# Decay attention in blocks of 64 tokens with a state in mid-chunk, and the second products of hidden group 0 in units of two banks

## The chip, the cores and the metric

The program runs on one core of a Trainium2 chip. The metric is the device time of one execution in microseconds (us), the median of three runs. TensorE (PE) does the matrix products, VectorE (DVE), ScalarE (ACT) and GpSimd (POOL) the elementwise work, and SyncE (SP) issues the DMA transfers. PEld stands for TensorE's weight loads.

## The reference

Two parts, cut to what matters. First an attention with a decay per head, in blocks of tokens with a running state (2 sequences of 768 tokens, 8 heads of 64 channels):

```python
for b in range(nb):                                  # block = 64 tokens
    intra = einsum('bhic,bhjc->bhij', qb, kb) * Dmask          # lam**(i-j), lower triangle
    intra = einsum('bhij,bhjd->bhid', intra, vb)
    inter = einsum('bhid,bhde->bhie', qb * lam_pow, kv_state)  # lam**(i+1)
    out[:, :, sl] = intra + inter
    kv_state = lam_block * kv_state + einsum('bhsd,bhse->bhde', kb * rev_pow, vb)
```

Its output is laid out as 1536 tokens by 512 channels. Two layers follow, each `(act(x @ w_in)) @ w_out` with 2048 hidden units, the first with Mish and the second with SiLU. The result does not depend on the size of the block, as long as the powers of lam are those of the distance between two tokens.

## The kernel before

**Numbers.** The products of the two layers are done in fp32r with each operand split into a high and a low part (`xh`, `xl`, `wh`, `wl`, `gh`, `gl`): three products for one, so 12 matmuls of 128x512 for one 128-wide slice of hidden units and one `t` (512 tokens). A weight is split by two passes on ACT (L95, L96), two on DVE (L123, L127), a cast on ACT (L167) and a subtraction on POOL (L168). The attention's products are plain fp32. Each of these matmuls stands in the trace as two.

**Attention.** There are N = 12 chunks of 128 tokens, six of a sequence. `emit_S` makes the scores of one chunk for 4 pairs of heads (8 matmuls, contraction over 64 channels, 128x128 each, into two banks `s`), and DVE multiplies them by `dmask` into `sm`. `emit_state` makes `pc` = keys times values (8 matmuls with 64 columns), which DVE adds to the decayed `state`. `emit_px` makes the state's part of the output and `emit_out` the scores' part (8 matmuls with 128 columns each, in one bank `px`), which ACT copies to `xh` and DVE completes with `xl`. ACT and POOL make the decayed keys `kd`, POOL the decayed queries `qd`.

**Order.** All engines' instructions stand in the order in which Python emits them (a manual schedule), and each engine runs its own list in that order. Chunks 0 to 3 (PH = 4) are done alone at the start. Then 12 steps follow (`t` over 3 groups of 512 tokens, `f` over the 4 hidden slices of group 0). Step i emits `emit_h(t, f)` (the first product of a slice, `ph`), then chunk n = i + 4 as long as n < 12, then, from step 2 on, the second product of the slice two steps back (`emit_o`, 12 matmuls into four banks `po` that stay open over four slices and are copied by ACT at the end, `evac`). Steps 0 to 7 hold a chunk, steps 8 to 11 none. After that the seven other groups of hidden units run as a list of items, with a faster algorithm (`Block`) for two of the three token groups. Its operands are sums of blocks of x, which `make_sums` lists and `run_sums` emits from step 8 on: 13 DVE operations of 128x1024.

**PSUM** has eight banks: two for `ph` (`ps_h`), four for `po` (`ps_o`), two for the attention (`ps_a`).

Of the kernel before, what the change touches and what calls it, by code (L numbers as in the profile page):

```python
# [17 lines left out]
def decay_attention_mish_silu_kernel(  # L18
# [8 lines left out]
    nc = tc.nc  # L27
# [5 lines left out]
    C = P  # L33
    NP = H // 2
# [13 lines left out]
    accp = ctx.enter_context(tc.tile_pool(name="accp", bufs=1))  # L48
# [5 lines left out]
    ps_o = ctx.enter_context(tc.tile_pool(name="ps_o", bufs=4, space=PSUM))  # L54
# [137 lines left out]
    ps_a = actx.enter_context(tc.tile_pool(name="ps_a", bufs=2, space=PSUM))  # L192


    states = [ac.tile([P, NP, D], F32, name=f"state{i}") for i in range(2)]

    def warm(n):
# [9 lines left out]
    unit = ac.tile([P, C], F32, name="unit")  # L207
    nc.gpsimd.memset(unit, 0.0)
    nc.gpsimd.affine_select(
        out=unit, in_=unit, pattern=[[1, C]], base=1 - C, channel_multiplier=1, compare_op=ALU.not_equal, fill=1.0  # L210
    )
# [27 lines left out]
    load_x()  # L239
    load_w(0, 0)  # L240
    load_x()
    load_w(1, 0)

    qd, kd, ss, sm, pxs = {}, {}, {}, {}, {}

    def emit_kd(n):
        if n < N and n % CPS < CPS - 1:
# [10 lines left out]
    def emit_qd(n):  # L258
        if n < N and n % CPS > 0:
            t = qd[n] = at.tile([P, NP, C], F32, tag="qd", name="qd")  # L260
            nc.gpsimd.tensor_tensor(out=t, in0=nat[n][1], in1=lamrow, op=ALU.mult)  # L261

    def emit_S(n, pool, tag, mask=True):
        if n >= N:
            return
        kT, qT, kn, vn = nat[n]
        ss[n] = [pool.tile([P, NP, C], F32, tag=tag, name=f"s{hh}") for hh in range(2)]
        for p in range(NP):
            for hh in range(2):
                r = slice(64 * hh, 64 * hh + 64)  # L270
                nc.tensor.matmul(ss[n][hh][:, p, :], lhsT=kT[r, p, :], rhs=qT[r, p, :], start=True, stop=True)  # L271
        if mask:
            emit_mask(n)

    def emit_mask(n):
        t = sm[n] = at.tile([P, 2, NP, C], F32, tag="sm", name="sm")
        for hh, s in enumerate(ss.pop(n)):
            nc.vector.tensor_tensor(out=t[:, hh], in0=s, in1=dmask[:, hh], op=ALU.mult)

    def emit_decay(n):  # L280

        if 0 < n % CPS < CPS - 1:
            nc.gpsimd.tensor_tensor(
                out=states[(n + 1) % 2], in0=states[n % 2],
                in1=lamrow[:, :, C - 1 : C].to_broadcast([P, NP, D]), op=ALU.mult,
            )

    def emit_state(n):
        c = n % CPS
        if c == CPS - 1:  # L290
            return
        vn = nat[n][3]
        early = PH <= n < PH + LAG
        pc = (ps_o if early else ps_a).tile([P, NP, D], F32, tag="o" if early else "a", name="pc")
        for p in range(NP):
            for hh in range(2):
                h = 2 * p + hh
                nc.tensor.matmul(  # L298
                    pc[64 * hh : 64 * hh + 64, p, :], lhsT=kd[n][:, h, :], rhs=vn[:, h, :], start=True, stop=True
                )  # L300
        new = states[(n + 1) % 2]
        if c == 0:
            nc.vector.tensor_copy(new, pc)
        else:
            nc.vector.tensor_tensor(out=new, in0=pc, in1=new, op=ALU.add)

    def emit_px(n):
        px = pxs[n] = (ps_h if n < PH else ps_a).tile([P, NP, C], F32, tag="h" if n < PH else "a", name="px")
        if n % CPS > 0:
            for p in range(NP):  # L310
                for hh in range(2):
                    r = slice(64 * hh, 64 * hh + 64)
                    nc.tensor.matmul(  # L313
                        px[r, p, :], lhsT=states[n % 2][r, p, :], rhs=qd[n][r, p, :],
                        start=(p == 0), stop=False, skip_group_check=True,
                    )

    def emit_out(n):
        px, vn = pxs.pop(n), nat.pop(n)[3]
        for p in range(NP):  # L320
            for hh in range(2):
                nc.tensor.matmul(  # L322
                    px[64 * hh : 64 * hh + 64, p, :], lhsT=vn[:, 2 * p + hh, :], rhs=sm[n][:, hh, p, :],
                    start=(n % CPS == 0 and p == 0), stop=(p == NP - 1), skip_group_check=True,
                )
        xslots.append(held.pop(("x", n)))
        xh, xl = x_tile(n // CPB)
        o = slice((n % CPB) * C, (n % CPB + 1) * C)
        nc.scalar.copy(xh[:, :, o], px)
        nc.vector.tensor_tensor(out=xl[:, :, o], in0=px, in1=xh[:, :, o].bitcast(F32), op=ALU.subtract)  # L330
# [10 lines left out]
    def bank(name):  # L341
        nbank[0] += 1
        if len(late) > 2 and nbank[0] % 2:
# [45 lines left out]
    def emit_o(t, n, first, last):  # L389
# [4 lines left out]
        if first:  # L394
            po[t] = [ps_o.tile([P, T], F32, tag="o", name="po") for j in range(4)]
# [19 lines left out]

    PIECES = [(j, slice(0, T)) for j in range(3)] + [(3, slice(0, T // 2)), (3, slice(T // 2, T))]
# [15 lines left out]
    def evac(mm, g, t):  # L432
        if g == 0:
            accs[mm, t] = (accp if t == 0 else late[1]).tile([P, 4, T], F32, tag="acc", name="acc")
# [42 lines left out]
    def make_sums(pool):  # L477
# [8 lines left out]
        fz = late[1].tile([P, 4, T], F32, tag="acc", name="fz")[:, 0:2]  # L486
        add, sub = ALU.add, ALU.subtract
        summing.extend([
            [tt(fx, a21[0], a22[0], add), tt(fx, fx, a21[1], add)],
            [tt(fx, fx, a22[1], add), cast(0, fx), tt(fz, *a11, add)],  # L490
            [low(0, fx), tt(fx, fx, fz, sub), cast(1, fx)],
            [tt(fz, fz, a21[0], sub), low(1, fx)],
            [tt(fz, fz, a21[1], sub), cast(2, fz), tt(fx, a12[0], fx, sub)],
            [low(2, fz), tt(fx, fx, a12[1], add), cast(3, fx)],
# [72 lines left out]
    loads = ["x", (2, 0), "x", (0, 1), "x", (3, 0), (1, 1), "x", (2, 1), (3, 1), "x", (4, 0), (5, 0)]  # L567
# [11 lines left out]
    spread = ps_a.tile([P, H], F32, tag="a", name="spread")  # L579
# [5 lines left out]
    dmask = ac.tile([P, 2, NP, C], F32, name="dmask")  # L585
    ages = dmask[:, :, :, C - 1]
    lamrow = ac.tile([P, NP, C], F32, name="lamrow")
    last = ac.tile([P, H], F32, name="last")
    nc.gpsimd.tensor_tensor(out=last, in0=lams, in1=unit[:, 0:1].to_broadcast([P, H]), op=ALU.mult)
    powers = ps_a.tile([P, NP, C], F32, tag="a", name="powers")  # L590
    for hh in range(2):
        for p in range(NP):
            h = H - 1 - (2 * p + hh)
            nc.vector.tensor_tensor_scan(
                out=dmask[:, hh, p], data0=lams[:, h : h + 1].to_broadcast([P, C]), data1=unit, initial=0.0,
# [3 lines left out]
    emit_S(0, ps_o, "o")  # L599
    for hh in range(2):  # L600
        for p in range(NP):
            h = H - 1 - (2 * p + hh)
            nc.tensor.matmul(
                powers[64 * hh : 64 * hh + 64, p, :], lhsT=last[:, h : h + 1].to_broadcast([P, 64]),
                rhs=dmask[:, hh, p], start=True, stop=True,
            )
    emit_kd(0)
    nc.scalar.copy(lamrow, powers)
    emit_qd(1)
    emit_state(0)  # L610
    emit_px(0)
    emit_out(0)
    emit_decay(1)
    emit_kd(1)
    emit_S(1, ps_o, "o")
    emit_px(1)
    emit_state(1)
    for n in range(PH):
        if n > 1:
            emit_state(n)  # L620
            emit_px(n)
        if n:
            if n < PH - 1:
                emit_S(n + 1, ps_o, "o")
            if n == PH - 2:
                run_split(2)
            emit_out(n)
            if n == PH - 1:
                emit_S(n + 1, ps_o, "o")
            if n == PH - 1:  # L630
                emit_kd(n + 1)
            emit_qd(n + 1)
            emit_decay(n + 1)
        if n == 1:
            for half in ((0, 0), (1, 0), (2, 0), (0, 1), (3, 0), (1, 1), (2, 1), (3, 1), (4, 0), (5, 0)):
                split_w(*half, half[0] > 3)
        pump()
        if n != PH - 2:
            run_split(2)
        run_pre(1 + (n == PH - 1), 0)  # L640
        run_parts()
        if n < PH - 2:
            emit_kd(n + 2)
        tick[0] += 1

    for i, (t, f) in enumerate(steps):
        n = i + PH
        if n == N:
            actx.close()
            late.append(ctx.enter_context(tc.tile_pool(name="ringt", bufs=2)))  # L650
            late.append(ctx.enter_context(tc.tile_pool(name="accq", bufs=NB - 1)))
            fctx = ExitStack()
            make_sums(fctx.enter_context(tc.tile_pool(name="ps_f", bufs=1, space=PSUM)))
# [4 lines left out]
        run_parts()  # L658
        if i < LAG or n >= N:
            run_split(2)  # L660
        emit_h(t, f, f == 0)
        if n < N:
            if i == 1:
                run_parts()
            emit_state(n)
            emit_px(n)
            if i < LAG:
                emit_S(n + 1, ps_o, "o")
            emit_out(n)
# [143 lines left out]
```

## Time and profile before

| | |
|---|---|
| time, median of 3 runs | 563.49 us (563.44 to 563.55) |
| profiled execution | 563.52 us, span 561.7 us |
| granted TensorE clock | 1.00 in every stretch |
| PE busy | 556.1 us (99%) |
| first `ph` product begins | 22.83 us |
| chunk steps end, step 8 begins | 90.68 us |

The span runs from the first to the last instruction; 1.8 us of the profiled execution lie outside it. Busy time on PE counts matmuls from their start to their modelled end, and they overlap, so that a busy PE does not say how fast it goes: for that the distance from one batch of matmuls to the next is read.

### The profile page before, as it was taken

Reading aid. Unit: us, or ns where it says so; the run is one execution under the profiler, and the core shown is the slowest. Engines: PE = TensorE matmul, PEld = TensorE weight load, DVE = VectorE, ACT = ScalarE, POOL = GpSimd, SP = SyncE. Lnnn points to the kernel's source line nnn. Section 1 sums busy time; section 2 is a strip of 40 time slices with the busy share of each in tenths; the row PEclk is TensorE's granted clock in tenths of the full one; section 3 lists DMA queues with packets and bytes.
Section 4 is the critical chain, followed back from the end, with each engine's and each line's share of the span. In section 5 each row is a group of like instructions: output and inputs, shape, how many; then the busy total and the mean of one; then the engine's idle time right before and its main releaser. Section 6 shows DMA issues by size and latency. Waiting matters only on the chain.

```text
span 561.7 us, 7611 instructions
## 1 busy us (share of the span) xinstructions
PE 556.1 (99%) x2956; PEld 454.6 (81%) x2956; DVE 312.3 (56%) x458; ACT 286.9 (51%) x538; POOL 164.1 (29%) x137
## 2 busy tenths in 40 slices
PE   9999999999999999999999999999999999999997
PEld 6877778887887888888888788888888888888885
DVE  4866536764467684446669882344634654455222
ACT  4676422863562763455546973656443654355120
POOL 4554512123034122312462652302322312303000
PEclk9999999999999999999999999999999999999999
DMA  8986600122022231212311141212320322100203
GB/s 301 405 271 224 226 1 1 49 93 84 1 76 75 69 118 39 75 39 80 109 38 37 41 150 41 70 39 87 101 75 2 109 78 73 41 0 1 75 7 144
DMA packets 14597, 49.77 MB, mean 89 GB/s; under 512 B 1633, under 2 KB 1889, under 8 KB 14561
## 3 DMA queue, kind: packets, MB, share of 16 engines
q1 hardware_dynamic: 14560, 49.29, 25.8%
q8 instruction: 23, 0.38, 0.3%
q14 instruction: 14, 0.11, 0.1%
HBM read 46.14 MB, written 3.15 MB: 88 GB/s over the span
## 4 chain that ended last, share of the span: by engine, by line
PE 95%; DMA 2%; SPq 1%; DVE 1%; POOL 0%; ACT 0%; issue 0%; DVEq 0%; POOLq 0%
PE po L409 46%; PE ph L382 20%; PE b L519 10%; PE a L519 7%; PE e L519 3%; PE c L519 3%; DMA xslot<-x 2%; PE px L322 2%; PE s L271 2%; PE px L313 1%; PE pc L298 1%; SPq L226 1%; DVE acc L440 1%; POOL wl L168 0%; POOL qd L261 0%
## 5 line engine op out<-in xcount | busy, mean ns | idle before, releaser
L168 POOL TENSOR_TENSOR wl<-dec,wh 128x512 fp32r<-128x512 f32 x64 | 85.2, 1333 | 270.6 <-ACT wh L167 233.6
L409 PE MATMUL po<-gh,wh 128*128 128x512 f32 x192 | 75.9, 395 | 0.1
L409 PE MATMUL po<-gh,wl 128*128 128x512 f32 x192 | 75.0, 390 | 0.1
L409 PE MATMUL po<-wh,gh 128*128 128x512 f32 (+1 forms) x193 | 75.0, 388 | 0.0
L409 PE MATMUL po<-wh,gl 128*128 128x512 f32 (+1 forms) x193 | 74.9, 388 | 0.0
L409 PE MATMUL po<-wl,gh 128*128 128x512 f32 (+1 forms) x193 | 74.9, 388 | 0.0
L366 DVE TENSOR_TENSOR gl<-ph,gh 128x512 fp32r<-128x512 f32 x40 | 27.5, 688 | 71.8 <-ACT ph L365 71.8
L365 ACT ACTIVATE gh<-ph 128x512 fp32r<-128x512 f32 x40 | 23.9, 598 | 80.5 <-PE ph L382 80.3
L382 PE MATMUL ph<-xh,wh 128*128 128x512 f32 x160 | 62.8, 395 | 0.0
L123 DVE SCALAR_TENSOR_TENSOR dec<-dec,slot 128x512 uint32<-128x512 uint32 x64 | 52.5, 820 | 17.4 <-ACT slot L96 16.0
L382 PE MATMUL ph<-xl,wh 128*128 128x512 f32 x160 | 60.8, 389 | 0.0
L440 DVE TENSOR_TENSOR acc<-po,acc 128x512 f32<-128x512 f32 (+1 forms) x73 | 45.7, 676 | 23.8 <-PE po L409 23.8
L167 ACT CAST wh<-dec 128x512 fp32r<-128x512 f32 x64 | 39.6, 619 | 37.4 <-DVE dec L127 37.0
L168 POOL TENSOR_TENSOR tl<-t,th 128x512 fp32r<-128x512 f32 x28 | 38.3, 1377 | 65.4 <-ACT th L167 63.9
L409 PE MATMUL po<-gl,wh 128*128 128x512 f32 x192 | 51.4, 389 | 0.0
L127 DVE SCALAR_TENSOR_TENSOR dec<-slot,dec 128x512 uint32<-128x512 uint32 x64 | 48.9, 764 | 1.7
L409 PEld LDWEIGHTS po<-gh,wh 128*128 128x128 f32 x192 | 36.0, 188 | 9.6 <-DVE acc L440 1.4
L382 PE MATMUL ph<-xh,wl 128*128 128x512 f32 x160 | 43.7, 389 | 0.0
L95 ACT ACTIVATE dec<-slot 128x512 f32<-128x512 f32 x64 | 42.7, 667 | 2.1 <-DMA slot<-w 2.1
L96 ACT ACTIVATE slot<-slot 128x512 uint32<-128x512 uint32 x64 | 42.7, 667 | 0.0
L409 PEld LDWEIGHTS po<-wh,gh 128*128 128x128 f32 x193 | 36.2, 188 | 7.7 <-issue 0.3
L409 PEld LDWEIGHTS po<-wl,gh 128*128 128x128 f32 x193 | 36.2, 188 | 7.5
(119 smaller groups left out, 946.7 us busy)
## 6 DMA issues: line engine op xcount, KB each, us to landing
slot<-w SPq DMA_DIRECT2D x64, 512.0 KB, 3.6
xslot<-x SPq DMA_DIRECT2D x24, 512.0 KB, 8.1
out<-acc SPq DMA_DIRECT2D x11, 256.0 KB, 2.1
out<-acc SPq DMA_DIRECT2D x2, 128.0 KB, 1.9
factors<-lam SPq DMA_DIRECT2D x1, 0.0 KB
```

The lines of the kernel that those rows point to most:

```text
L95: nc.scalar.activation(decs[n, i].bitcast(F32), high.bitcast(F32), AF.Copy, scale=2.0**-112)
L96: nc.scalar.activation(low, low, AF.Copy, scale=TOP3, bias=2.0**-21 - 0.5)
L123: nc.vector.scalar_tensor_tensor(out=d, in0=d, scalar=3, in1=low, op0=ALU.logical_shift_left, op1=ALU.bitwise_or)
L127: nc.vector.scalar_tensor_tensor(out=d, in0=high, scalar=0x80000000, in1=d, op0=ALU.bitwise_and, op1=ALU.bitwise_or)
L167: nc.scalar.copy(hi, f)
L168: nc.gpsimd.tensor_tensor(out=lo, in0=f, in1=hi.bitcast(F32), op=ALU.subtract)
L365: nc.scalar.activation(to, ps, AF.Mish if mm == 0 else AF.Silu)
L366: later.append(lambda: nc.vector.tensor_tensor(out=gl, in0=ps, in1=gh.bitcast(F32), op=ALU.subtract))
L382: nc.tensor.matmul(ph, lhsT=wi[wsel][:, kk * P : (kk + 1) * P], rhs=xt[xsel][:, kk, :], start=(i == 0), stop=(i == 3 * KD - 1),)
L409: nc.tensor.matmul(po[t][j][:, c], lhsT=lhsT, rhs=rhs, start=(first and wsel + gsel == 0), stop=(last and gsel == 1 and c.stop == T),)
L440: nc.vector.tensor_tensor(out=acc[:, j, c], in0=po[t][j][:, c], in1=acc[:, j, c], op=ALU.add)
L519: nc.tensor.matmul(self.b[dst], lhsT=w[ws][:, kk * P : (kk + 1) * P], rhs=x[xx][:, kk, :], start=(start and i == 0), stop=(i == 5), skip_g ...
```

## The change

Attention works on half chunks: L = 64 tokens. All its matmuls contract over 64 rows into 64 columns of output partitions and move 64 columns, so that each uses one quarter of TensorE's array, and there are 16 of them where there were 8. The state is kept at the end of the chunk (`states`) and in its middle (`mids`); POOL makes `fades`, the state decayed by half a chunk. `emit_pc` makes both halves' `pc`, `emit_state` the next state, `emit_intra` the scores' part and `emit_inter` the states' part of `px`. The first product of the chunk that begins a sequence has no state in its first half only. In the steps the order is `emit_h`, intra, `pc`, then the second product, inter, and the scores of the next chunk.

The second products of group 0 are emitted as `emit_u`: a unit takes two slices and two of the four output blocks, 12 matmuls into two banks, which are emptied at once (ACT copies the first two units of a `t` to `acc`, DVE adds the others to it). `ps_o` has two banks, and the sums get PSUM for both of their operands and 12 smaller groups in another order. At the start the whole of chunk 3 is loaded ahead of the first weights, and the weights' order differs by one place.

```diff
-    def emit_S(n, pool, tag, mask=True):
+    def emit_S(n, pair=False):
...
         for p in range(NP):
+            for c in range(2):
+                for hh in range(2):
+                    r = inner[hh]
+                    nc.tensor.matmul(
+                        s[hh][rows[c], p], lhsT=kT[r, p, rows[c]], rhs=qT[r, p, half[c]], start=True, stop=True
+                    )
...
+    def emit_pc(n):
+        c0, ends = n % CPS == 0, n % CPS == CPS - 1
...
+        for p in range(NP):
+            for c in range(1 if ends else 2):
+                for hh in range(2):
+                    h = 2 * p + hh
+                    nc.tensor.matmul(
+                        pc[inner[hh], c, p], lhsT=kd[n][rows[c], h], rhs=vn[rows[c], h], start=True, stop=True
+                    )
+        mid = mids[n % 2]
+        if c0:
+            nc.vector.tensor_copy(mid, pc[:, 0])
+        else:
+            nc.vector.tensor_tensor(out=mid, in0=pc[:, 0], in1=fades[n % 2], op=ALU.add)
...
+    def emit_inter(n):
+        for c in (1, 0)[: 1 if n % CPS == 0 else 2]:
+            state = (states, mids)[c][n % 2]
+            for p in range(NP):
+                for r in inner:
+                    nc.tensor.matmul(
+                        pxs[n][1][c][r, p], lhsT=state[r, p], rhs=qd[n][r, p, c],
...
+    def emit_u(t, u, between=None):
+        js, fs = (2 * (u % 2), 2 * (u % 2) + 1), (2 * (u // 2), 2 * (u // 2) + 1)
...
+        order = ((0, 0, 0), (0, 0, 1), (1, 0, 0), (0, 1, 0), (1, 0, 1), (1, 1, 0))
+        passes = [(fs[k], j, ws, gs) for k, ws, gs in order for j in range(2)]
+        for i, (f, j, ws, gs) in enumerate(passes):
+            if between and i == len(passes) // 2:
+                between()
...
+        def leave():
+            for j in range(2):
+                if u < 2:
+                    nc.scalar.copy(acc[:, js[j], :], banks[j])
+                else:
+                    nc.vector.tensor_tensor(out=acc[:, js[j], :], in0=banks[j], in1=acc[:, js[j], :], op=ALU.add)
...
+            leave = emit_u(*divmod(i - LAG, 4), close if ends else None)
+            if n < N and not ends:
+                emit_inter(n)
+            if n < N:
+                emit_S(n + 1, True)
+            if n < N and not ends:
+                emit_out(n)
+            if n < N:
                 run_parts()
+            leave()
...
-        run_sums(1 + (i > len(steps) - 3))
+        run_sums(1 + (n < N + 2))
```

On PE, step 4 (chunk 8) reads as follows before, from the end of `ph` on; S of the next chunk closes it.

```order
L382 MATMUL ph<-xl,wh_281 128x512 x4
L298 MATMUL pc<-xslot_100,kd 64x64 x8
L313 MATMUL px<-qd,state_98 64x128 x8
L322 MATMUL px<-sm,xslot_100 64x128 x8
L409 MATMUL po<-gh,wh_610 128x512
...
L409 MATMUL po<-gl,wh_610 128x512 x4
L271 MATMUL s_836<-xslot_101 128x128
L271 MATMUL s_837<-xslot_101 128x128
```

The same step of the change (`px` from `sm` is intra, `px` from `mid` and `state` is inter):

```order
L428 MATMUL ph<-xl,wh_399 128x512 x4
L346 MATMUL px<-sm,xslot_104 64x64 x16
L313 MATMUL pc<-xslot_104,kd 64x64 x16
L474 MATMUL pu<-gh,wh_803 128x512 x2
L474 MATMUL pu<-gl,wh_803 128x512 x2
L474 MATMUL pu<-gh,wh_930 128x512 x2
L474 MATMUL pu<-gh,wl_804 128x512 x2
L474 MATMUL pu<-gl,wh_930 128x512 x2
L474 MATMUL pu<-gh,wl_931 128x512 x2
L357 MATMUL px<-qd,mid_100 64x64 x8
L357 MATMUL px<-qd,state_98 64x64 x8
L296 MATMUL s<-xslot_105 64x64 x16
```

The attention's products stand in two blocks of one shape where they stood in two blocks of four shapes, and the state's part has moved behind the second product, next to S.

On ACT, in step 2 before, the cast of the weights of the fourth slice (`wh_481`) that step 3's `ph` reads, and what stands around it:

```order
L365 ACTIVATE gh<-ph 128x512
L365 ACTIVATE ph<-ph 128x512
L329 CAST xh<-px 128x4x128
L256 ACTIVATE kd<-xslot_103,dmask 128x64 x4
L167 CAST wh_481<-dec 128x512
```

In the change the same cast is that of `wh_796`:

```order
L411 ACTIVATE gh<-ph 128x512
L411 ACTIVATE ph<-ph 128x512
L168 CAST wh_689<-dec 128x512
L264 ACTIVATE kd<-xslot_107,dmask 128x64 x4
L375 CAST xh<-px 128x4x128
L168 CAST wh_796<-dec 128x512
```

It is still behind the copy of the chunk's `px`, but that `px` is now finished only after the second product.

On DVE, from step 8 on before (`t` are weights' sums, `fx` and `fz` the sums of x, `gl` the low part that the second product reads):

```order
L430 TENSOR_TENSOR fx<-xh 128x1024
L430 TENSOR_TENSOR fx<-fx,xl 128x1024
L153 TENSOR_TENSOR t_1087<-dec 128x256
L153 TENSOR_TENSOR t_1087<-dec,t_1087 128x256
L366 TENSOR_TENSOR gl<-ph,gh 128x512
L430 TENSOR_TENSOR fx<-fx,xl 128x1024
L430 TENSOR_TENSOR fz<-xh,xl 128x1024
L366 TENSOR_TENSOR gl<-ph,gh 128x512
```

And in the change, from step 8 to the start of step 10:

```order
L484 TENSOR_TENSOR acc<-pu,acc 128x512 x2
L505 TENSOR_TENSOR fx<-xh 128x1024
L505 TENSOR_TENSOR fx<-fx,xl 128x1024
L154 TENSOR_TENSOR t_1587<-dec 128x256
L154 TENSOR_TENSOR t_1587<-dec,t_1587 128x256
L412 TENSOR_TENSOR gl<-ph,gh 128x512
L484 TENSOR_TENSOR acc<-pu,acc 128x512 x2
L505 TENSOR_TENSOR fx<-fx,xl 128x1024
L505 TENSOR_TENSOR fz<-xh,xl 128x1024
...
L412 TENSOR_TENSOR gl<-ph,gh 128x512
```

Each step's sums now stand behind two additions that wait for the end of the step's unit.

## Rows read from the trace of the kernel before

**Rows 1.** Page: the span, and each engine's busy time.

```profile
span 561.7 us, 7611 instructions
PE 556.1 (99%) x2956; PEld 454.6 (81%) x2956; DVE 312.3 (56%) x458; ACT 286.9 (51%) x538; POOL 164.1 (29%) x137
```

**Rows 2.** Page: the chain that ended last, by engine.

```profile
PE 95%; DMA 2%; SPq 1%; DVE 1%; POOL 0%; ACT 0%; issue 0%; DVEq 0%; POOLq 0%
```

**Rows 3.** Windows: busy PE, PEld, DVE, ACT, POOL; PEclk, DMA share, GB/s.

```profile
0.00:22.83 22.83, 21.55 (x286) 16.57 (x286) 13.75 (x28) 11.89 (x31) 10.42 (x18) 1.00 0.90 341
22.83:44.07 21.24, 21.24 (x209) 16.88 (x209) 14.82 (x22) 14.85 (x34) 11.90 (x13) 1.00 0.82 281
90.52:139.96 49.44, 49.31 (x217) 40.47 (x216) 32.27 (x38) 27.87 (x49) 12.51 (x9) 1.00 0.20 64
```

**Rows 4.** Chain in order of time: start us, length us, what.

```profile
22.83 2.94 PE ph L382 x12
...
44.07 2.95 PE ph L382 x12
...
53.74 2.95 PE ph L382 x12
56.69 0.62 PE pc L298 x16
57.30 1.02 PE px L313 x16
58.32 1.02 PE px L322 x16
59.35 2.97 PE po L409 x12
62.31 1.09 PE s L271 x16
...
82.74 2.95 PE ph L382 x12
...
90.68 2.72 PE ph L382 x12
```

**Rows 5.** Timeline of PE at the start: start us, busy us, shape, count.

```profile
14.10 1.09 PE L322 MATMUL px<-sm,xslot 128*64 128x128 f32 x16
15.02 0.64 PE L298 MATMUL pc<-xslot,kd 128*64 128x64 f32 x16
15.59 1.09 PE L313 MATMUL px<-qd,state 64*64 64x128 f32 x16
```

**Rows 6.** Timeline of PE, chunk 0's `pc` among `powers`.

```profile
8.52 0.27 PE L603 MATMUL powers<-dmask,last 128*64 128x128 f32 x1
8.52 0.22 PE L298 MATMUL pc<-xslot,kd 128*64 128x64 f32 x1
8.63 0.27 PE L603 MATMUL powers<-dmask,last 128*64 128x128 f32 x1
```

**Rows 7.** Timeline of the first weights and chunk 3 at the start.

```profile
13.20 0.42 DVE L305 TENSOR_TENSOR state<-pc,state 128x256 f32<-128x256 f32 x1 [0.30 <-PE pc L298]
...
17.65 1.06 ACT L256 ACTIVATE kd<-xslot,dmask 128x64 f32<-128x64 f32 x4 [0.67 <-DMA xslot<-x]
...
19.32 0.69 ACT L95 ACTIVATE dec<-slot 128x512 f32<-128x512 f32 x1
...
21.18 0.62 ACT L167 CAST wh<-dec 128x512 fp32r<-128x512 f32 x1 [0.60 <-DVE dec L127]
21.78 0.59 ACT L329 CAST xh<-px 128x512 fp32r<-128x512 f32 x1
```

**Rows 8.** Timeline of DVE from step 8 on.

```profile
89.01 0.68 DVE L366 TENSOR_TENSOR gl<-ph,gh 128x512 fp32r<-128x512 f32 x1
89.61 0.41 DVE L153 TENSOR_TENSOR t<-dec 128x256 f32<-128x256 f32 x1
...
91.66 1.23 DVE L430 TENSOR_TENSOR fx<-fx,xl 128x1024 f32<-128x1024 f32 x1
```

More of the change, by code (lines that the diff above doesn't have):

```diff
@@ L280, in emit_decay @@
[L280 to L285, printed above, removed]
-            )
[L288 to L291, printed above, removed]
+        t = sm[n] = at.tile([P, 2, NP, L], F32, tag="sm", name="sm")
+        if pair:
+            both = ps_a.tile([P, 2, T], F32, tag="xy", name="s")[:, :, 0 : NP * L].rearrange("q hh (p i) -> q hh p i", p=NP)
+            s = [both[:, hh] for hh in range(2)]
+        else:
+            s = [ps_o.tile([P, NP, L], F32, tag="o", name=f"s{hh}") for hh in range(2)]
@@ new lines, in emit_state, with emit_intra @@
+    def emit_state(n):
+        pc, mid = pcs.pop(n), mids[n % 2]
+        if n % CPS == CPS - 1:
+            return
+        for p in range(NP):
+            nc.vector.scalar_tensor_tensor(
+                out=states[(n + 1) % 2][:, p], in0=mid[:, p], scalar=lamrow[:, p, L - 1 : L], in1=pc[:, 1, p],
+                op0=ALU.mult, op1=ALU.add,
+            )
+        emit_fade(n + 1)
+    def emit_intra(n):
+        if n < PH and n % 2 == 0:
+            pxs[n] = None, [ps_h.tile([P, NP, L], F32, tag="h", name=f"px{i}") for i in range(2)]
+        else:
+            both = ps_a.tile([P, 2, T], F32, tag="zw", name="px")[:, :, 0 : NP * L]
+            both = both.rearrange("q c (p i) -> q c p i", p=NP)
+            pxs[n] = both, [both[:, i] for i in range(2)]
@@ L307, in emit_px @@
[L307 to L330, printed above, removed]
+            for c in range(2):
+                for hh in range(2):
+                    nc.tensor.matmul(
+                        pxs[n][1][c][inner[hh], p], lhsT=vn[rows[c], 2 * p + hh], rhs=sm[n][rows[c], hh, p],
+                        start=(p == 0), stop=(p == NP - 1 and c == 0 and n % CPS == 0), skip_group_check=True,
+                    )
@@ new lines, in emit_inter, with emit_out @@
+    def emit_inter(n):
+        for c in (1, 0)[: 1 if n % CPS == 0 else 2]:
+            state = (states, mids)[c][n % 2]
+            for p in range(NP):
+                for r in inner:
+                    nc.tensor.matmul(
+                        pxs[n][1][c][r, p], lhsT=state[r, p], rhs=qd[n][r, p, c],
+                        start=False, stop=(p == NP - 1), skip_group_check=True,
+                    )
+        del nat[n]
+        xslots.append(held.pop(("x", n)))
+    def emit_out(n):
+        both, px = pxs.pop(n)
+        xh, xl = x_tile(n // CPB)
+        o = n % CPB * C
+        if both is None:
+            parts = [(px[c], slice(o + L * c, o + L * c + L), "q p i -> q p i") for c in range(2)]
+        else:
+            parts = [(both.rearrange("q c p i -> q p c i"), slice(o, o + C), "q p (c i) -> q p c i")]
+        for src, cols, form in parts:
+            sizes = {"c": 2} if "c" in form else {}
+            hi, lo = [a[:, :, cols].rearrange(form, **sizes) for a in (xh, xl)]
+            nc.scalar.copy(hi, src)
+            nc.vector.tensor_tensor(out=lo, in0=src, in1=hi.bitcast(F32), op=ALU.subtract)
@@ L689, in decay_attention_mish_silu_kernel @@
         tick[0] += 1
-    fills = [lambda s=s: emit_o(*s, False, s[1] == GF - 1) for s in steps[-LAG:]]
+    fills = [lambda u=u: emit_u(NB - 1, u)() for u in range(4 - LAG, 4)]
     for g in range(1, 2 * NG):
```

253 lines of the change are left out of this document (140 added, 113 removed).

## Prediction

> **What bounds the kernel now.** The page first: PE is busy 556.1 of 561.7 us [rows 1], and the chain that ended last is 95% PE [rows 2]. So the time changes where PE's own list gets shorter, or where PE is made to wait. Busy time cannot show the first, since overlapping matmuls count as busy whatever their pace, so I read the distances in the chain [rows 4]. A batch of 12 matmuls of 128x512 takes 2.72 us among its like and 2.95 to 2.97 beside attention. In step 4 the attention's four batches (`pc` 0.62, `px` 1.02 twice, S 1.09) take 3.75 of 9.67 us. Then the windows [rows 3], to see who could make PE wait: from the first `ph` to the fourth ACT is busy 14.9 of 21.2 us and DVE 14.8, from step 8 to the first `Block` DVE is busy 32.3 of 49.4. The granted clock is 1.00, the upper level of 2.4 GHz, throughout.
>
> **The prices of attention on PE.** Between two batches of one array form, `px` takes 0.92 us to the next batch (14.10 to 15.02), against 1.02 where a change of form follows too. `pc` takes 0.57 (15.02 to 15.59) where only its end meets another form, and 0.62 where both ends do [rows 4, 5]. So entering a form costs 0.05, leaving it 0.10, and the bare work is 0.87 for 128 columns and 0.47 for 64. Each batch is 16 matmuls of the trace that run two at a time: 0.47/8 = 58 ns for a pair of 64 columns. Two things follow for the change. Its batches stay in one form (quarters), so the 0.15 falls once per block. And its S, intra and `pc` are 32 matmuls of 64 columns that address four different quarters. If four run at once as two do now, a batch takes Q = 8 x 58 ns = 0.47 us, and if only two do, 0.94. Inter uses two quarters on the diagonal and takes 0.94 in either case (0.47 for one half).
>
> No row has four at once. What speaks for it: chunk 0's `pc` runs in one half of the columns while `powers`, ahead of it in the program, is still running in the other half, starts 8.52 and 8.52 [rows 6]. So each part of the array takes its own work as it comes, and the two halves do not slow each other. I take 0.47, the pace of the nearest row, and keep 0.94 as the other end.
>
> **Steps 3 to 7.** Steps 4, 5 and 6 go from 9.67 us to two big batches at 2.96 and two blocks, 0.15 + 2 Q and 0.15 + 0.94 + Q: 5.92 + 1.09 + 1.56 = 8.57, which is -1.10 each. Step 3 has inter in the middle of the unit, so a third block and one more pair of edges on the big matmuls (2.96 - 2.72 = 0.24): 2.96 + 2.72 + 0.48 + 1.09 + 1.09 + 0.62 = 8.96, -0.71. Step 7 was 7.94 (82.74 to 90.68), as it had no `pc` and no S; now it has half a `pc` on two quarters (0.47): 2.96 + 2.72 + 0.36 + 1.09 + 1.09 = 8.22, +0.28. Together **-3.7 us** (with 0.94, 13 batches x 0.47 = 6.1 more, +2.4).
>
> **Steps 0 to 2.** These took 21.24 us (22.83 to 44.07). By the same prices step 0 and step 1 are 2.96 + 0.15 + 3 Q + 0.94 = 5.46 each and step 2 is 2 x 2.96 + 0.15 + 0.94 + 0.15 + 0.47 + 0.47 = 8.10, so 19.02, or -2.2. I don't count all of it. In steps 0 and 1 inter needs `mid`, which DVE makes after `pc`: a DVE operation of 0.42 that began 0.12 after `pc`'s end [rows 7], and some 0.1 back to PE, 0.64 against the 0.47 of S that lies between; with a weight pass on DVE ahead of it more. I take 0.3 for each step. And the order on ACT shows the cast for step 3's `ph` behind the copy of `px`, which now ends only with inter: 0.59 + 0.62 behind it [rows 7], less S and its edge (0.62), so `ph` waits 0.6. Left: **-1.0 us**. Bounds: -2.2 if nothing waits, 0 if ACT, whose list is the same length and has less time, eats all of it.
>
> **The start.** The first `ph` begins at 22.83. Chunk 3's second half landed for ACT at 17.65 [rows 7]; now the first weights stand in that place of the queue, since all of chunk 3 goes ahead of them. From there: two ACT passes (19.32 and the next, 0.57 apart, 1.2 together), the two halves of chunk 2's `px` behind them on ACT (0.6), their low parts and `mid` on DVE (0.5 + 0.4), two weight passes (1.4), the cast (0.6): 17.6 + 4.7 = 22.3, and 0.2 to `ph`. That is what it was: **0**, with -1.5 (one transfer of 0.52 MB earlier, at the mean of 341 GB/s [rows 3]) and +1.5 (the DVE passes as slow as in the busiest rows, and waits between) as bounds. Half the work on S and the mask at the start lies in the shadow of the loads and counts nothing; without that shadow it would be worth some 0.5 us a chunk.
>
> **The sums.** From step 8 on two additions (0.61 each, the distance of two such operations [rows 8]) stand on DVE behind the unit's end and ahead of the sums, where the first sum began with step 8. Follow it from the end of step 9's unit: 0.2 to get there, 1.2 for the additions, two sums of 1.2, two `t` 0.8, `gl` 0.6: 5.2 us. Step 10's unit reads this `gl` at its ninth matmul, after 2.72 + 8 x 0.227 (a twelfth of 2.72) = 4.5: PE waits 0.7. Then DVE has low, `fz`, two weight passes, `gl`, two sums, two weight passes and the next `gl`: 4 x 1.2 + 4 x 0.7 + 2 x 0.6 = 8.8. PE comes for it after the last four matmuls of step 10, step 11's two batches and eight matmuls: 0.9 + 5.44 + 1.8 = 8.1, a wait of 0.7. **+1.3 us** (0 if the sums run ahead, +3 if ACT's casts in between come late). Behind that six batches of 2.72 stand ahead of the first `Block`, and the last four groups of the sums are less than that, so nothing more is late. The copies that ACT loses to DVE here lie under PE's batches. Past there the instructions and the number of banks are the same.
>
> **The sum.** -3.7 - 1.0 + 0 + 1.3 = -3.4 us. The profiled execution took 563.52 us, as the median of 563.49: **560.1 us**. Its own range, from the bounds that don't change Q, is 557.5 to 562.
>
> **The rivals.**
> *Only two at a time (slower).* The rows on average never show more than one small matmul per 29 ns (16 in 0.47, rows 5). If that is not the columns' time but the pace at which PE takes small matmuls, then Q is 0.94: steps 3 to 7 +2.4, steps 0 to 2 +1.6 (8 batches x 0.47, less the waits that this covers), sums +1.3: +5.3, 568.8 us. It decides from Q = 0.63 on, where 21 batches x 0.16 make up 3.4. Against it stand the starts at one moment [rows 6] and that the pair's pace follows its columns, 58 ns for 64 and 109 for 128 [rows 5]. Chance 0.15.
> *A floor in between (slower).* A pace per matmul halfway between 29 ns and the 14.6 that four at once would need is 22 ns, Q = 0.70: -3.4 + 21 x 0.23 = +1.4, 564.9 us. Speaks for it: 64 small matmuls follow each other in each block, where no row has more than 48. Chance 0.10. The Trainium skill states such a floor in "TensorE: Matmul & The Clock Gate", section "Wait — 56ns, not 53.3ns?": start to start never drops below about 25 ns however few columns; by that figure, an estimate, a batch is 32 x 25 = 0.8 us and the time about 567. The rows agree in so far as their mean is 29 ns, though two of them start at one moment [rows 6]. The Trainium skill's "TensorEngine Tiling (Array Packing)", Tiling Modes, counts four independent tiles of 64x64, which would give my forecast; no row here shows four.
> *Three of four on average, or DVE and ACT later than I count (no change).* Q about 0.6, or the sums at +3 and steps 0 to 2 at 0: 562.4 to 564.6. Chance 0.15.
> *The early gain stays too (faster than forecast).* No waits for `mid` and the cast, start 1.5 earlier, sums for nothing: -7.4, 556.1 us. Against it: ACT's and DVE's orders. Chance 0.10.
>
> **How the numbers follow.** The forecast has 0.50. A measurement of this kernel tells 0.2% (1.1 us) from no change. Faster: 0.50 + 0.10 = 0.60; the same 0.15; slower 0.25. For 8 in 10 I leave out most of the two-at-a-time case above (0.15) and the lowest end (0.04): 557 to 566.5 us.
>
> **What will show it.** `pc` and S in the steps at 0.5 to 0.6 us for 32 matmuls if four run at once, 1.0 or more if not. Step 4 to step 5, `ph` to `ph`, 8.57. The first `ph` at 22.5 to 23. A wait of PE before step 3's `ph` with ACT's cast as its end. Two waits of 0.7 inside the units of step 10 and of the item after step 11, released by `gl` on DVE. The forecast is wrong if Q is above 0.63, if the clock falls below 1.00 in the pauses of PE at the start (between chunk 3's `pc`, near 18 us, and its inter, near 20, by the count above), where a big batch would take twice its 2.72 us, or if inter waits for `qd` or `mid` in every step.

## The result: 1.5% slower, and where the profile after puts it

The changed kernel takes 572.05 us (median of four runs, 570.03 to 573.54) against 563.52 of the kernel before beside it: a ratio of 1.0149, 95% interval 1.0117 to 1.018. The forecast of 560.1 us, its range and its sign were wrong. The profiled execution of the changed kernel took 571.89 us.

The page after, lines that answer to [rows 1, 2], with the granted clock by fortieths of the span and the queue that brings instructions:

```profile
span 570.1 us, 9241 instructions
...
PE 553.2 (97%) x3724; PEld 451.6 (79%) x3724; DVE 327.6 (57%) x510; ACT 288.4 (51%) x548; POOL 170.7 (30%) x144
...
PEclk9789999999999999999999999999999999999999
...
q8 instruction: 29, 0.48, 0.4%
...
PE 86%; issue 5%; DVE 3%; DMA 2%; POOL 2%; ACT 1%; SPq 0%; DVEq 0%; POOLq 0%; ACTq 0%
```

PE is busy 2.9 us less than before, and the span is 8.4 us longer. PE's share of the chain fell from 95% to 86%, and 5% is now "issue", in which the engine waits for nothing that the profile shows (7.7 us of it are PE's own, below; most of the rest lies behind step 8, where the chain loses the thread while PE is busy). Of the PEclk digits, the first four stand for the first 57 us, and two of them are below 9.

The windows after, with the columns of [rows 3], cut at the first `ph`, at the `ph` of steps 3 and 8, and at the first `Block`:

```profile
0.00:30.68 30.68, 21.64 (x557) 16.82 (x557) 13.46 (x46) 9.86 (x29) 10.12 (x20) 0.86 0.83 311
30.68:53.60 22.92, 20.56 (x400) 16.32 (x400) 18.71 (x34) 18.25 (x43) 16.86 (x16) 0.97 0.63 204
53.60:96.92 43.32, 42.96 (x713) 33.90 (x713) 27.56 (x49) 20.76 (x48) 18.30 (x18) 1.00 0.39 137
96.92:148.30 51.38, 50.42 (x218) 40.24 (x217) 38.85 (x50) 27.30 (x47) 11.57 (x9) 1.00 0.19 62
```

Stage by stage, against [rows 3, 4]: the start is 30.68 us in place of 22.83 (+7.85, forecast 0), steps 0 to 2 are 22.92 in place of 21.24 (+1.68, forecast -1.0), steps 3 to 7 by the chain (53.60 to 97.08) 43.48 in place of 46.61 (-3.13, forecast -3.7), and from step 8 to the first `Block` 51.38 in place of 49.44 (+1.9, forecast +1.3). That is 8.3 of the 8.4 us. In the start PE is busy for as long as before (21.64 and 21.55 us) with about twice the records (557 and 286), and idle 9 us.

PE's waits in the changed kernel (engine, operation, what it waited for: us in total, times, longest us):

```profile
PE pc L313 <- issue: 6.4, 3, 2.3
PE ph L428 <- ACT wh L168: 1.4, 2, 1.1
PE px L357 <- DVE mid L320: 1.0, 3, 0.6
PE px L346 <- issue: 0.9, 1, 0.9
PE pu L474 <- ACT acc L482: 0.5, 1, 0.5
PE s L296 <- issue: 0.4, 1, 0.4
```

The kernel before had no wait on "issue". The chain after, in order of time, shows where these stand, with two batches of step 4 at the end (start us, length us, what):

```profile
18.16 0.43 PE pc L313 x10
18.59 2.05 issue
20.64 0.50 PE pc L313 x17
...
21.78 1.49 PE px L357 x26
...
24.45 0.43 PE pc L313 x8
24.88 2.07 issue
26.94 0.58 PE pc L313 x17
...
30.68 3.76 PE ph L428 x12
...
40.38 0.43 PE px L346 x17
40.81 0.93 issue
...
66.14 0.62 PE px L346 x32
66.77 0.47 PE pc L313 x32
```

PE stops in the middle of a batch, after 14 and 12 of the 32 matmuls of a `pc` (the ones ahead of those 10 and 8 stand among the last of `px`), with no semaphore that it waits for, and goes on 2 us later. Around these stops everything is slow too: `px` at 21.78 takes 1.49 us for 26 matmuls (step 4: 0.90, 70.19 to 71.09), and the first `ph` 3.76 us in place of 2.94. Beside that the arithmetic units do what was forecast: `px` and `pc` of 32 matmuls take 0.62 and 0.47 us in step 4.

What the stops have in common is a count. The windows of the changed kernel between them (the x behind PE's busy time is the number of its matmul records):

```profile
0.00:11.92 11.92, 10.52 (x220) 6.69 (x221) 4.99 (x21) 4.37 (x13) 4.29 (x13) 1.00 0.78 275
14.20:18.59 4.39, 4.18 (x127) 3.85 (x126) 2.54 (x8) 2.24 (x9) 3.58 (x5) 0.61 1.02 372
20.60:24.88 4.28, 4.12 (x126) 3.79 (x127) 2.70 (x9) 0.65 (x2) 0.62 (x1) 0.67 1.04 419
26.90:40.81 13.91, 12.69 (x253) 10.33 (x253) 10.37 (x23) 10.14 (x23) 8.74 (x8) 0.88 0.53 171
41.73:62.59 20.86, 19.67 (x382) 15.34 (x382) 18.84 (x29) 14.94 (x35) 13.91 (x12) 1.00 0.79 258
```

127, 126, 2 x 126.5 and 3 x 127.3 records lie between one stop and the next. The instruction queue moved 29 packets of 16 KB for 3724 records, 128 each (23 for 2956 in the kernel before, which is 128 as well). Five of its packets start in the trace at 11.78, 18.22, 24.44, 39.5 and 60.57 us, and PE goes on at 14.25, 20.64, 26.94, 41.73 and 62.95: each time 2.2 to 2.5 us behind the first byte. The three between them (28.17, 44.27 and 51.54) came 3.4 us or more ahead of their place in the count, and PE did not stop there. So **theory 1** was: PE runs dry of instructions. The change nearly doubles them in the start (557 records for 286), where the queues are full of x and weights. **Rivals**: the order of the loads, with chunk 3 ahead of the first weights, and ACT and DVE behind it; and the granted clock by itself.

### The profile page after: what moved, and what is told of

The parts are those of the page before. It is cut to its first block, busy times and chain, and to the rows that moved or that the text cites. A ratio compares the mean times of both kernels' runs of the same rounds, so it can differ in the third digit from the quotient of the medians.

```text
span 570.1 us, 9241 instructions
## 1 busy us (share of the span) xinstructions
PE 553.2 (97%) x3724; PEld 451.6 (79%) x3724; DVE 327.6 (57%) x510; ACT 288.4 (51%) x548; POOL 170.7 (30%) x144
## 4 chain that ended last, share of the span: by engine, by line
PE 86%; issue 5%; DVE 3%; DMA 2%; POOL 2%; ACT 1%; SPq 0%; DVEq 0%; POOLq 0%; ACTq 0%
PE po L455 39%; PE ph L428 16%; PE b L599 10%; PE a L599 7%; PE e L599 3%; PE c L599 3%; PE pu L474 3%; PE px L357 2%; DMA xslot<-x 2%; PE px L346 1%; POOL wl L169 1%; PE pc L313 1%; DVE dec L128 1%; PE s L296 1%; DVE acc L515 1%
## 5 line engine op out<-in xcount | busy, mean ns | idle before, releaser
L124 DVE SCALAR_TENSOR_TENSOR dec<-dec,slot 128x512 uint32<-128x512 uint32 x64 | 54.7, 855 | 15.6 <-ACT slot L97 14.3
L168 ACT CAST wh<-dec 128x512 fp32r<-128x512 f32 x64 | 39.5, 617 | 35.0 <-DVE dec L128 34.6
L455 PE MATMUL po<-gh,wl 128*128 128x512 f32 x144 | 56.3, 391 | 0.3 <-POOL wl L169 0.2
L455 PE MATMUL po<-gh,wh 128*128 128x512 f32 x144 | 56.5, 392 | 0.1
L128 DVE SCALAR_TENSOR_TENSOR dec<-slot,dec 128x512 uint32<-128x512 uint32 x64 | 53.1, 830 | 1.7
L455 PEld LDWEIGHTS po<-wh,gl 128*128 128x128 f32 x193 | 36.2, 188 | 7.4
L455 PE MATMUL po<-gl,wh 128*128 128x512 f32 x144 | 38.5, 389 | 0.0
```

The source lines that it names most:

```text
L124: nc.vector.scalar_tensor_tensor(out=d, in0=d, scalar=3, in1=low, op0=ALU.logical_shift_left, op1=ALU.bitwise_or)
L128: nc.vector.scalar_tensor_tensor(out=d, in0=high, scalar=0x80000000, in1=d, op0=ALU.bitwise_and, op1=ALU.bitwise_or)
L168: nc.scalar.copy(hi, f)
L455: nc.tensor.matmul(po[t][j][:, c], lhsT=lhsT, rhs=rhs, start=(first and wsel + gsel == 0), stop=(last and gsel == 1 and c.stop == T),)
```

## The experiments

**e1, the count moved.** 40 tiny matmuls ahead of chunk 0's S.

```diff
+    def tiny(n):
+        t = ps_h.tile([64, 8, 64], F32, tag="h", name="tiny")
+        for _ in range(n):
+            nc.tensor.matmul(t[:, 0, 0:8], lhsT=zeros, rhs=zeros[:, 0:8], start=True, stop=True)
     warm(6)
+    tiny(40)
     emit_S(0)
```

> The changed kernel with 40 tiny TensorE matmuls (64x64 weights, 8 columns, on zeros) more, ahead of chunk 0's S, where TensorE has nothing to do but wait for the first x. Theory 1 (TensorE runs dry of instructions: they come in pieces of 16 KB, 127 matmul records of the trace apart, and a piece that is asked for late stops TensorE wherever it is in its list): the three waits of 2.0 to 2.3 us that end nobody's work, now inside pc of chunks 0, 1 and 2 at the 221st, 348th and 474th matmul record, come at the same records counted from the program's start, so 40 records earlier in the work: inside px of chunks 0, 1 and 2, and none is left in pc. Rival (the load order and the busy DVE and ACT make the start late, and the waits belong to pc's own operands): the waits stay in pc at the same matmuls of it. In both the first ph moves by under 2 us.

Measured: 573.46 us in one run, first `ph` at 33.31. Its three largest waits on nothing, in the list of waits:

```profile
PE px L351 <- issue: 7.1, 3, 3.8
```

and its windows up to the first of them, from there to the second, and to the third:

```profile
0.00:12.92 12.92, 11.69 (x221) 7.64 (x221) 4.01 (x18) 4.40 (x14) 4.20 (x12) 1.00 0.80 287
14.30:17.30 3.00, 2.77 (x126) 2.50 (x127) 1.74 (x7) 0.07 (x1) 1.51 (x2) 1.00 1.03 388
21.05:25.73 4.68, 4.63 (x127) 4.45 (x126) 1.94 (x7) 0.17 (x1) 0.18 (x1) 0.50 1.03 414
```

The three stops are at the 221st record and 126 and 127 records on, and no longer in `pc` but in `px`, 40 records earlier in the work. Where PE stops is set by how many instructions it has behind it and by nothing in them. The first `ph` was 2.6 us later, more than the 2 expected, as one of the stops took 3.8 us. This settles theory 1 for the place of the waits; it leaves open what makes a piece late.

**e2, emptier queues.** The slots of x are given back later, so that no load is issued between the first six and the end of chunk 2.

```diff
-        xslots.append(held.pop(("x", n)))
+        freed.append(held.pop(("x", n)))
+        if n >= PH - 2:
+            xslots.extend(freed[::-1])
+            freed.clear()
```

> The changed kernel with the x slots of chunks 0 and 1 given back only with that of chunk 2, so that no load is issued between the six that the program begins with and the end of chunk 2: the DMA queues fall idle at about 17 us instead of running on to 28. The output is unchanged. Theory 1 (a piece of TensorE's instructions takes 3.8 to 4.9 us from the asking to its first packet while the data queues are full, and 1.2 us when they are empty): the second and above all the third wait on nothing (2.05 and 2.07 us, at 18.6 and 24.9) shrink to under 0.7 us each and the first ph comes 2 to 4 us earlier than 30.7. Rival (the start is late by the load order): the waits stay at 2 us and the first ph stays within 1 us, or is later as the loads of chunk 4 are later.

Measured: 566.48 us, ratio 1.0049 (1.0034 to 1.0064); the first `ph` at 26.51, 4.2 us earlier than in the changed kernel. Its waits on nothing:

```profile
PE pc L314 <- issue: 3.0, 3, 1.8
```

and its windows between the three stops:

```profile
14.70:18.53 3.83, 3.80 (x127) 3.66 (x126) 1.97 (x8) 0.65 (x2) 0.75 (x2) 0.64 0.73 275
19.05:22.31 3.26, 3.09 (x126) 2.70 (x127) 2.55 (x10) 2.17 (x6) 1.81 (x3) 1.00 0.55 176
```

The stops are at the same records and take 1.75, 0.57 and 0.69 us. The queues were not empty but less full: the DMA share of the two windows is 0.73 and 0.55, against 1.02 and 1.04 in the changed kernel. The last two pieces began to arrive at 16.76 and 20.32, some 65 and 75 records ahead of the place where they were needed; in the changed kernel it was 2 or 3 records (at 18.22 and 24.44). So a piece is late because its transfer stands behind x and weights: full queues brought one every 6.2 to 6.8 us in the changed kernel and in e1, and 6.6 in the kernel before, where PE did not stop. What is left of the late start in e2, 3.7 us, is its stops (3.0) and a slower piece behind the first (3.83 for 3.26). The second window also has the price of the clock by itself: 126 records take 3.09 us at a granted clock of 1.00 and 4.12 to 4.18 where its mean is 0.61 to 0.67.

**e3 and e8, instructions alone.** The kernel before with 64 tiny matmuls behind the `pc` of chunks 0 to 3; in e8 two of them can run at once.

```diff
+        for j in range(64 if n < PH else 0):
+            a, b = slice(0, 64), slice(64 * (j % 2), 64 * (j % 2) + 64)
+            nc.tensor.matmul(wide[b, NP, 0:8], lhsT=zeros[a], rhs=zeros[a, 0:8], start=True, stop=True)
```

(e3 has `wide[0:64, NP, 0:8]`, `zeros` and `zeros[:, 0:8]` there; `wide` is `pc`'s bank in full.)

> The kernel before with 64 tiny TensorE matmuls (64x64 weights, 8 columns, on zeros, into an unused half of pc's bank) behind the pc of each of chunks 0 to 3, so that TensorE has as many instructions in a chunk there as the changed kernel has, and nothing else of the change. Theory 1: waits on nothing of about 2 us appear in the start, one per 127 records, and the first ph comes 3 to 8 us later than 22.8, more than the tiny matmuls' own busy time. Rival (load order, DVE, ACT): the first ph is later by the tiny matmuls' own time at most (64 of some 25 ns, 1.6 us a chunk, most of it under the wait for x), so by 0 to 2 us, and no such wait appears.

Measured: 573.17 us in one run, the first `ph` at 32.50, but only one wait on nothing, of 0.6 us, at the 349th record. The tiny matmuls took 31.7 ns each, 2.0 us a chunk, and those of three chunks at least stood in the way: 6 to 8 of the 9.7 us are theirs. So e3 decides nothing, and the waits of 2 us that were expected did not come: PE was slow enough for its pieces, which came every 6.1 and 6.7 us. That is why there is e8.

> As e3 (the kernel before with 64 tiny TensorE matmuls behind the pc of each of chunks 0 to 3), but the tiny matmuls use one half of the rows and the two halves of the columns in turn, so that two can run at once: some 16 ns each in place of 32, 1.0 us a chunk. Theory 1: in the changed kernel a piece of 127 records lasts 6.3 us from one wait's end to the next (4.3 us of work and 2.0 of waiting) while the queues are full; here the work of 128 records is 4.1 + 1.0 us, so waits on nothing of about 1 us each come at two or three of the records near 221, 348 and 474, and the first ph at 28 to 31 us. Rival (instructions are no limit): no such wait, and the first ph at 22.8 plus at most 4.1, 27 us.

Measured: 572.16 us in one run, the first `ph` at 31.47. Its waits on nothing:

```profile
PE pc L307 <- issue: 3.0, 2, 2.4
```

and its windows up to the first stop and from it to the second:

```profile
0.00:14.75 14.75, 13.77 (x221) 9.88 (x221) 6.35 (x16) 5.59 (x16) 6.02 (x13) 1.00 0.84 306
15.40:19.52 4.12, 4.09 (x127) 3.81 (x128) 2.36 (x4) 1.26 (x3) 2.48 (x3) 1.00 1.03 409
```

Two stops, of 0.67 and 2.37 us, at the 221st record and 127 on, in a kernel that has nothing of the change but, nearly, its number of instructions. There were two and not three; a piece came every 6.3 us here as well (13.04, 19.35, 25.69), and behind the second stop PE was slow enough. The first `ph` is 8.6 us later than before, a little more than expected: 3.0 of it are the stops and some 4.1 at most the tiny matmuls; the rest was not taken apart.

**e4 to e6, the change without its start.** e4 computes chunks 0 to 3 as before, in the order and with the loads of before up to the first `ph`, and the rest in blocks of 64; the masks of 64 are cut out of those of 128. So it undoes the start as a whole, and not the number of instructions alone.

```diff
+    smC = accp.tile([P, 4, T], F32, tag="acc", name="smC")
+    dmaskC = accp.tile([P, 4, T], F32, tag="acc", name="dmaskC")[:, 0:2].rearrange("q a (p i) -> q a p i", p=NP)
+    lamrow = lamrowC[:, :, 0:L]
...
+            if n == PH - 1:
+                emit_S(n + 1)
+                emit_kd(n + 1)
+                emit_qd(n + 1)
+                emit_fade(n + 1)
+            else:
+                old_qd(n + 1)
+                old_decay(n + 1)
...
+        elif n == PH - 2:
+            for r in range(2):
+                nc.gpsimd.tensor_copy(
+                    dmask[L * r : L * r + L], dmaskC[L * r : L * r + L, :, :, L - L * r : C - L * r]
+                )
```

> The changed kernel with chunks 0 to 3 computed as before (products of 128 tokens, the masks and powers of 128, the order and the loads of before up to the first ph), chunks 4 to 11 in blocks of 64 as in the changed one, and the units. Theory 1: the first ph is back at 22.8 to 23.5 us with no wait on nothing ahead of it; steps 0 to 2 take 21 to 22 us, steps 3 to 7 43.5, and what comes behind is 2.0 longer than before, so in all 561 to 564 us, 8 to 11 less than the changed kernel. Rival (the lateness is in the steps too, as the instructions there are as many): more waits on nothing turn up in steps 0 to 4 and the time stays above 566.

Measured: 564.52 us (twelve runs, 563.0 to 566.06), ratio 1.0013 (1.0003 to 1.0024), 0.5 above what was expected. The first `ph` is at 22.38 with no wait on nothing ahead of it, 8.3 us earlier than in the changed kernel. Its one large wait is my own doing (the copies on POOL are late, and two weight passes stand ahead of `mid` on DVE): 2.6 us in step 0, for `mid`. The windows over that wait and over the `ph` behind it show what it costs:

```profile
27.00:29.60 2.60, 0.03 (x2) 0.04 (x2) 2.57 (x5) 2.52 (x6) 1.32 (x2) 1.00 0.70 268
...
30.60:35.20 4.60, 4.60 (x19) 3.32 (x16) 3.79 (x6) 2.00 (x5) 4.25 (x4) 0.63 0.84 297
```

A `ph` of 2.95 us takes 4.6 at a mean clock of 0.63. e5 takes the wait away.

```diff
+        if n == PH - 3:
+            for r in range(2):
+                nc.gpsimd.tensor_copy(
+                    dmask[L * r : L * r + L], dmaskC[L * r : L * r + L, :, :, L - L * r : C - L * r]
+                )
         if n < PH - 2:
             old_kd(n + 2)
-        elif n == PH - 2:
...
         run_later()
-        if i == 0:
-            run_split(2)
         emit_h(t, f, f == 0)
```

> The kernel of e4 (chunks 0 to 3 as before, the rest in blocks of 64) with its two flaws mended: the small mask is copied out of the large one a chunk earlier on GpSimd, ahead of chunk 3's kd, and step 0 has no weight pass on VectorE ahead of its mid. Theory (a wait of TensorE of 2 us costs its own length and then slow work at a lower granted clock): the wait of 2.6 us for mid in step 0 goes below 0.7, the ph of step 1 takes 2.95 us and not 4.6, and the time falls by 3.5 to 4.5 us, to 560 to 561. Rival (the clock has nothing to do with that wait): only the wait itself goes, 562.

Measured: 562.70 us (eleven runs, 562.25 to 563.50), ratio 0.9986 (0.9977 to 0.9995). The wait in step 0 is 0.15 us, and the `ph` of step 1 takes 3.0 us: the slow `ph` went with the wait, as the theory had it. In all only 1.8 us are gained, half of what was expected, and the time is nearer to the rival's 562, because a wait of 0.95 for `mid` in step 1 and one of 1.06 for the cast ahead of step 3's `ph` (0.7 in e4) stand there now. e6 also changes the order behind the steps.

```diff
-            items = [[fills[0], wos[1]], [hs[0], wos[2]], [fills[1], wos[3], lambda: sum_pair(3)], [hs[1]]]
-            items += [[us[0]], [hs[2]], [us[1]], [hs[3]], [us[2]], [us[3]]]
+            items = [[hs[0], wos[1]], [fills[0], wos[2]], [hs[1], wos[3], lambda: sum_pair(3)], [fills[1]]]
+            items += [[hs[2]], [us[0]], [hs[3]], [us[1]], [us[2]], [us[3]]]
```

> e5, and in the part behind the steps the second products of group 0 no longer follow each other directly: the items run ph, unit, ph, unit, ph instead of unit, ph, unit, ph. Theory (with two banks for a unit, the second of two neighbouring units waits 0.45 us for ScalarE's copies, and after any wait TensorE's next large matmuls are slower, 0.37 us in all): that wait and its wake go, 0.5 to 1.0 us less than e5. Rival (VectorE sets the pace of this part): the same work on VectorE is late somewhere else, and the time is within 0.3 us of e5.

Measured: 560.51 us (five runs, 560.14 to 560.97), ratio 0.9948 (0.9935 to 0.9962): faster than both kernels, and 2.2 less than e5, more than twice the 1.0 that was expected at most. The same four windows as above, of e6:

```profile
0.00:22.53 22.53, 21.00 (x302) 16.27 (x302) 13.64 (x28) 11.49 (x29) 11.24 (x20) 1.00 0.90 339
22.53:44.64 22.11, 19.80 (x400) 15.53 (x400) 19.13 (x34) 17.01 (x41) 17.41 (x16) 1.00 0.84 296
44.64:87.43 42.79, 42.79 (x712) 33.91 (x713) 27.97 (x49) 20.74 (x48) 18.28 (x18) 1.00 0.40 139
87.43:136.85 49.42, 49.26 (x218) 40.46 (x216) 39.65 (x52) 28.26 (x48) 12.92 (x10) 1.00 0.20 65
```

The last stage is 49.42 us as in [rows 3] (49.44), 2.0 less than in the changed kernel: not one wait went but three, those for ACT's copies (0.45) and two inside `po` (0.22 for POOL's `wl` and 0.12), each with slow matmuls behind it, the wake. The timeline of PE over the first of them in the changed kernel shows the wake (start, busy, what; pairs of matmuls):

```profile
118.22 0.62 PE L474 MATMUL pu<-gl,wh 128*128 128x512 f32 x2
118.68 0.61 PE L474 MATMUL pu<-gh,wl 128*128 128x512 f32 x2
119.74 0.99 PE L474 MATMUL pu<-gh,wh 128*128 128x512 f32 x2 [0.45 <-ACT acc L482]
120.57 0.63 PE L474 MATMUL pu<-gl,wh 128*128 128x512 f32 x2
```

A pair lasts 0.46 us from start to start; the one behind the wait lasts 0.83, 0.37 more, at a granted clock of 1.00. Behind the two shorter waits it is 0.1 more.

**e7, the load order.** The changed kernel with one line moved back.

```diff
     load_x()
+    load_w(0, 0)
     load_x()
-    load_w(0, 0)
     load_w(1, 0)
```

> The changed kernel with one thing undone: the first weights are loaded ahead of chunk 3 of x again, as before. Theory 1 (the start is late because TensorE's instructions come late): the three waits on nothing stay at 2 us each and the first ph stays within 1 us of 30.7, the time within 1.5 us of the changed kernel. Rival (the start is late by the order of the loads): the first ph comes 2 us or more earlier.

Measured: 571.60 us, ratio 1.0144 (1.013 to 1.0158). The waits on nothing ahead of the first `ph` are 2.46, 2.30 and 1.61 us, again in `pc`, and that `ph` is at 32.33, 1.65 us later than in the changed kernel, more than the 1 us that theory 1 allowed for. The rival is out: undoing the order gains nothing in the start, and the time is that of the changed kernel (570.51 to 572.74 against 570.03 to 573.54).

**e9, the cast first.** e6 with one exchange on ACT in step 2.

```diff
+            if i == LAG:
+                run_parts()
             if n < N and not ends:
                 emit_inter(n)
```

> The kernel of e6 with one pair exchanged on ScalarE in step 2: the cast of the weights for step 3's ph ahead of the copy of px, no longer behind it. Theory A (the ph of step 3 waits 1.0 us for that cast because the copy of px, and with it inter, is ahead of it): the wait falls to 0.4 or less and the time by 0.6 to 1.2 us. Theory B (the cast waits for VectorE's weight pass, which is slow beside GpSimd, 1.65 us against 0.69): the wait stays, and the time is within 0.3 us of e6.

Measured: 560.63 us, ratio 0.995 (0.9936 to 0.9964), the same as e6, and the wait of step 3's `ph` for the cast is still 1.05 us. The copy of `px` was not what held the cast. Theory B fits, as far as it says that the weight pass holds it: in e6 the weight pass ahead of that cast starts on DVE at 42.29 and takes 1.65 us (43.94), and the cast follows at 43.97.

## Why the prediction was wrong, step by step

**Q and the prices of attention: right.** Four quarters do run at once: 32 matmuls of 64 columns take 0.47 us (`pc` of step 4), 14.6 ns each, and in the records the four start 6 to 7 ns apart, every 58 ns. The floor of some 25 ns from start to start that the Trainium skill states in "TensorE: Matmul & The Clock Gate", section "Wait — 56ns, not 53.3ns?", does not hold here between matmuls on different quarters. The four independent tiles that the Trainium skill has in "TensorEngine Tiling (Array Packing)", Tiling Modes, agree with the trace. Both rivals on Q fall.

**Steps 3 to 7, -3.7: right.** Steps 4 to 6 take 8.57, 8.53 and 8.54 us (forecast 8.57). The changed kernel loses 0.6 of the gain in step 3 (9.56 us), where a stop on nothing of 0.36 us stands (62.59). In e6, without it, step 3 takes 8.97 (forecast 8.96), and the stage 42.79 against 46.52 by the same starts before (44.00 to 90.52): -3.73.

**The start, 0: this step failed.** I followed x, the weights, ACT and DVE to the first `ph` and took PE's own half of the change for nothing ("Half the work on S and the mask at the start lies in the shadow of the loads and counts nothing"). I counted the time of the matmuls and not their number. PE's instructions come in pieces of 127 records beside x and weights; with full queues a piece comes every 6.2 to 6.8 us, and the blocks of 64 use one up in 3 us at full clock. The trace of before had both numbers. Its pieces start at 13.99 and 20.63 us, and these are its windows between (columns of [rows 3]):

```profile
14.20:18.60 4.40, 4.40 (x80) 4.04 (x82) 3.10 (x6) 2.69 (x7) 1.50 (x4) 1.00 1.02 402
18.60:22.80 4.20, 3.91 (x69) 3.30 (x65) 3.84 (x6) 3.47 (x9) 2.93 (x3) 1.00 1.03 407
```

A matmul on the edge counts in both; in one window it is 145 records in 8.6 us, so PE used a piece up in 7.5 us with the queues as full: slow enough, by a little. The mechanism is shown by e1 (the place), e2 (the full queues) and e8 (instructions alone), and e4 to e6, with the whole start undone, get it back (22.4 to 22.6). The size, from the rows: three stops, 6.45 us together; two pieces that follow at the lower clock, 1.0 us longer each by e2's second window. These 8.5 us are more than the 7.85, presumably since PE would have waited for x a part of that time; that part was not measured by itself. The Trainium skill tells of these pieces in "Runtime: NRT & Kernel Launch", section "Instruction fetch mechanics": blocks of 16 KiB, fetched by a queue of the sequencer's own while the block before runs, at a cost that is mostly hidden. The 29 packets of 16 KB agree with the first part of that; the stops of 2 us do not agree with the last.

**The clock.** "If the clock falls below 1.00 in the pauses of PE at the start" stood among the things that would break the forecast, and it did: after the stops of 2.0 to 2.3 us the granted clock is at its lower level, 1.2 GHz, for part of the next piece (means of 0.61 and 0.67), and after the one of 0.93 it stays at 1.00. The prediction saw that the clock could fall in the start, but not what would make PE pause. It is a consequence: e4 makes the same fall with a wait for `mid`, e5 removes it with that wait.

**Steps 0 to 2, -1.0: wrong sign.** +1.68 in the changed kernel, of it 0.93 for a stop on nothing, 0.8 for the first `ph` at the lower clock, and 1.07 for the wait ahead of step 3's `ph`, which I had put at 0.6. In e6, where neither of the first two occurs, the stage is still 22.11, +0.87 and outside my bounds of -2.2 and 0: the waits of 0.95 for `mid` and 1.03 for the cast. What I mis-sized is the weight passes on DVE: this part of my sum has none ahead of the cast, and its other parts have them at 0.7 us each. The chain of the changed kernel has two of 1.70 and 1.66 us in this stage, beside a busy POOL, and the second of them leads to the cast and to step 3's `ph`:

```profile
51.25 1.66 DVE dec L128
...
52.93 0.63 ACT wh L168
...
53.60 3.02 PE ph L428 x12
```

The prediction had this wait from the copy of `px` on ACT. e9 shows for e6 that the order on ACT is not the cause; that POOL is what slows DVE was not tried.

**The sums, +1.3: right in sign, 1.9 measured, mostly by other waits.** The wait for `gl` in step 10's unit is there, 0.16 for a forecast 0.7. At the second place, behind step 11, the wait has another end: two units follow each other there on two banks, and PE waits 0.45 for ACT's copies. What I left out is these waits, the two inside `po` and the wake: 0.37 us behind the wait for the copies, 0.1 behind each of the others. e6 brings the stage back to its old length with a change of order alone.

**The rivals.** None of them was what happened; the slower side was expected from Q or from sums that come late, and it came from the number of instructions. The prediction's own range, 557.5 to 562, is narrower than its bounds, which add up to 556.1 and 564.3, and its text doesn't say why; 572 lies outside either.

## What to carry to other kernels

Where work is cut into more and smaller matmuls, count the instructions as well as the time: find in the trace how often the instruction queue delivers a piece while the data queues are full (6.2 to 6.8 us here), and compare that with the time in which PE uses one up (3 us). Keep such blocks for stages in which large matmuls lie between them, as in steps 4 to 6, which have no such stop. A wait of PE is priced with what follows it, the slow matmuls behind it and, after the long ones here, the lower clock.

## What the runs showed that was not expected

- PE stopped up to 3.8 us (e1) for its own instructions, in the middle of a batch, with no semaphore in sight; the trace calls it "issue".
- The packets of the instruction queue, 16 KB each, took as little as 0.9 us themselves; the time lies around them: 6.2 to 6.8 us from one to the next with full queues (4.5 and 3.6 in e2), and 2.2 to 2.5 us from the first byte until PE goes on.
- After a wait of 0.45 us, at a clock of 1.00, the next two large matmuls took 0.83 us in place of 0.46; behind waits of 0.12 to 0.22 us it was 0.1 more. Why, these runs don't say.
